# First half products of two dense chunks ahead of their loop, a two-bank integer decode, and later loads from a third buffer

## The chip, the cores and the metric

The program runs on one core of one Trainium2 chip. The metric is the device time in microseconds (us) of one execution, the median of the runs shown. A profiled execution gives the trace; its span runs from the first to the last instruction.

## The reference, cut to what matters

Three stages run one after the other: a linear attention with a decay per channel, a dense layer with an ELU, and a mixture of experts that sends each token to one expert.

```python
def _attn_ref(r, k, v, w, u):                 # (4, 8, 768, 48) each, u (8, 48)
    for t in range(S):
        cur = np.einsum('bhd,bhe->bhde', u[None] * kt, vt)
        y[:, :, t] = np.einsum('bhd,bhde->bhe', rt, state + cur)
        state = wt[:, :, :, None] * state + np.einsum('bhd,bhe->bhde', kt, vt)

def _moe_ref(x, w_in, w_out):                 # x (3072, 384), w_in (384, 2048), w_out (2048, 384)
    h = x @ w_in
    g = np.where(h > 0.0, h, alpha * (np.exp(np.minimum(h, 0.0)) - 1.0))
    return (g @ w_out).astype(np.float32)

def _moe2_ref(x, modality_id, w_gate, modality_bias, w1, w2):
    logits = x @ w_gate + modality_bias[modality_id]
    e_idx = np.argmax(logits, axis=1)
    ...
    for e in range(E):                        # 8 experts, 384 -> 1024 -> 384
        h = np.maximum(x[mask] @ w1[e], 0.0)
        out[mask] = gate_w[mask, None] * (h @ w2[e])
```

`w_in` and `w_out` come in as 64-bit floats and are turned into 32-bit ones on the chip.

## The kernel before, in words

The 3072 tokens are 24 tiles of 128 tokens: tile `i` holds chunk `c` of batch `b`, with `i = 4c + b`. Two tiles make one of 12 groups of 256 tokens.

**Attention** has four steps for each tile. `A1` turns the decays (buffer `lw`) into running products `RK` (a scan on VectorE, L358, then a reciprocal on ScalarE and VectorE, L361 to L364, that works in a PSUM bank). `A2` scales r and k by them (GpSimd, L409). `A3` multiplies them against each other (TensorE, L449) and masks the result (VectorE, L458). `A4` multiplies that with v (L492), adds up `y` (VectorE, L509), splits it into a high and a low half-precision part `x` (ScalarE L516, GpSimd L518) and transposes `x` into `xT` (L385 on TensorE and L386 on ScalarE for tiles 0 to 3, a DMA transpose on SyncE's queue for the others). `upd` keeps the state (L528). From tile 8 on, token rows of r and k (buffer `ld`) take the place of a TensorE product.

**The dense layer** goes through a group's 256 tokens in 8 chunks of 256 hidden columns. `ffn_in(g, u_)` makes 18 products of 256 columns each (L546) into one bank `psf`: two halves `z_` of 128 hidden columns, three parts of the 384 input channels, three products for the high and low parts. ScalarE and VectorE then make the ELU (L553, L554, L555) and ScalarE and GpSimd the two half-precision parts in `ring` (L557, L344). Two units later `ffn_out` multiplies them with `wo` (12 products of 384 columns, L570) into two of the three `pso` banks.

**The weights of the dense layer** come as 16 pieces: 8 of `w_in` and 8 of `w_out`, in the order of `SEQ`: in 0, in 1, in 2, out 0, in 3, out 1, and so on. `prep_` decodes one piece of 768 columns from 64 to 32 bits in six VectorE operations of 384 columns, by way of the bank `pso2` (L292, L293, L294, twice), and ScalarE and GpSimd then scale it and split it (L306, L309, L310). Only group 0 waits for this; the later groups find the weights in place.

**PSUM** has eight banks: two with the tag `f`, three with `a`, and the three `pso`. What `ffn_out` leaves free of a `pso` bank (`SC`) holds small data, such as `Z128`, the decay at the end of a tile (L372, read in L367).

**Order.** The Python code lays the attention steps and the dense units out in one list by the numbers `LEAD`, `LAGS` and `U_`, and a scheduler with a cost model then sets the order on each engine when the kernel is built. At run time each engine takes its instructions strictly in that order. SyncE issues the loads and the DMA transposes from one queue, in order.

Buffers: `psum(tag)` gives the next bank of a tag, `b2`, `p2`, `lw_` and the like are pools with a fixed number of buffers, and a pool that is closed hands its memory to the next one. The pool `LD[0]` is opened after unit 10 in the memory of the decode buffers.

## Time and profile before

| what | before |
|---|---|
| median of 3 runs | 743.87 us (741.7 to 748.42) |
| the profiled execution | 743.09 us |
| its span | 741.3 us |
| granted TensorE clock over the span | 0.993 |
| busy: TensorE, VectorE, ScalarE, GpSimd | 703.3, 506.0, 492.1, 408.3 us |

The profiled execution lasted 743.09 us, of which the span is 741.3 us and 1.79 us lie around it. TensorE is busy for 95% of the span, the others for 55 to 68%. A busy TensorE is not one at its peak, so the waits of TensorE and the spacing of its products tell more than the share.

### The profile page before, as it was taken

Reading aid. Unit: us, or ns where it says so; the run is one execution under the profiler, and the core shown is the slowest. Engines: PE = TensorE matmul, PEld = TensorE weight load, DVE = VectorE, ACT = ScalarE, POOL = GpSimd, SP = SyncE. Lnnn points to the kernel's source line nnn. Section 1 sums busy time; section 2 is a strip of 40 time slices with the busy share of each in tenths; the row PEclk is TensorE's granted clock in tenths of the full one; section 3 lists DMA queues with packets and bytes.
Section 4 is the critical chain, followed back from the end, with each engine's and each line's share of the span. In section 5 each row is a group of like instructions: output and inputs, shape, how many; then the busy total and the mean of one; then the engine's idle time right before and its main releaser. Section 6 shows DMA issues by size and latency. Waiting matters only on the chain.

```text
span 741.3 us, 17669 instructions
## 1 busy us (share of the span) xinstructions
PE 703.3 (95%) x6769; PEld 534.1 (72%) x6769; DVE 506.0 (68%) x1073; ACT 492.1 (66%) x959; POOL 408.3 (55%) x414
## 2 busy tenths in 40 slices
PE   4889999999999999999999999998997999999984
PEld 4767777777777777777777777776775777777763
DVE  5999974575756675657556645776794897667751
ACT  3578875677666677766666755476754887667752
POOL 5878898878677778778767650021053243321221
PEclk9999999999999999999999999999999999999998
DMA  9865442463324442354231201189449999989820
GB/s 301 260 232 188 129 129 66 124 145 86 100 68 105 125 100 69 93 112 98 78 80 56 33 13 34 54 286 275 144 164 284 341 370 330 249 244 272 267 77 13
DMA packets 89059, 114.77 MB, mean 155 GB/s; under 512 B 60709, under 2 KB 67018, under 8 KB 88964
## 3 DMA queue, kind: packets, MB, share of 16 engines
q1 hardware_dynamic: 84512, 102.75, 49.0%
q0 software_dynamic: 3456, 10.24, 4.6%
q8 instruction: 57, 0.93, 0.5%
q10 hardware_dynamic: 996, 0.53, 0.3%
q14 instruction: 38, 0.31, 0.2%
HBM read 90.29 MB, written 9.84 MB: 135 GB/s over the span
## 4 chain that ended last, share of the span: by engine, by line
PE 41%; DMA 18%; issue 13%; DVE 12%; POOL 9%; ACT 7%; POOLq 0%; DVEq 0%; SPq 0%; ACTq 0%
PE psf L546 13%; PE pso L570 13%; DMA out_dram<-ob,idxb 7%; DMA SG<-in_w_dram 4%; PE pso L907 4%; PE psf L887 3%; POOL ring L344 2%; DMA ld<-in_rk_dram 2%; DVE W L877 2%; DVE sti L294 1%; DVE RK L358 1%; PE psa L452 1%; POOL lk L409 1%; DVE pso L292 1%; DVE pso L293 1%
## 5 line engine op out<-in xcount | busy, mean ns | idle before, releaser
L546 PE MATMUL psf<-xT,wi 128*128 128x256 f16 x1728 | 209.3, 274 | 4.0 <-DVE e L555 1.9
L570 PE MATMUL pso<-wo,ring 128*128 128x384 f16 x1152 | 210.2, 326 | 2.0 <-ACT wo L309 0.7
L546 PEld LDWEIGHTS <-wi 128*128 128x128 f16 x1728 | 165.4, 98 | 31.1 <-issue 3.4
L570 PEld LDWEIGHTS <-ring 128*128 128x128 f16 x1152 | 109.8, 98 | 64.6 <-POOL ring L344 1.8
L344 POOL TENSOR_TENSOR ring<-e,ring 128x512 f16<-128x512 f32 x80 | 92.8, 1162 | 52.3 <-ACT ring L557 50.8
L555 DVE SCALAR_TENSOR_TENSOR e<-e,psf 128x512 f32<-128x512 f32 x96 | 65.7, 684 | 76.8 <-ACT e L554 70.9
L907 PE MATMUL pso<-W,gg 128*128 128x384 f16 x624 | 111.7, 326 | 2.5 <-DVE gg L344 1.4
L887 PEld LDWEIGHTS <-W 128*128 128x128 f16 x1008 | 93.6, 99 | 23.1 <-issue 3.8
L557 ACT ACTIVATE ring<-e 128x512 f16<-128x512 f32 x96 | 60.1, 626 | 48.2 <-DVE e L555 48.0
L907 PEld LDWEIGHTS <-gg 128*128 128x128 f16 x624 | 60.3, 98 | 37.1 <-DVE gg L344 2.1
L918 POOL DMA_INDIRECT out_dram<-ob,idxb x20 | 26.0, 1301 | 91.4 <-DVE ob L917 42.6
L553 ACT ACTIVATE e<-psf 128x512 f32<-128x512 f32 x96 | 56.6, 590 | 27.2 <-PE psf L546 23.1
L554 ACT ACTIVATE e<-e,nel 128x512 f32<-128x512 f32 x96 | 69.1, 720 | 2.3
L877 DVE SCALAR_TENSOR_TENSOR W<-SG,W 128x768 f16<-128x768 f32 x56 | 52.8, 956 | 19.2 <-ACT W L875 19.1
L887 PE MATMUL psf<-XM,W 128*128 128x256 f16 (+1 forms) x540 | 62.3, 266 | 1.4 <-ACT mt L893 1.3
L877 DVE SCALAR_TENSOR_TENSOR W<-wi,W 128x768 f16<-128x768 f32 x56 | 52.3, 954 | 13.1 <-ACT W L875 11.9
L875 ACT ACTIVATE W<-SG 128x768 f16<-128x768 f32 x56 | 45.8, 838 | 20.5 <-DMA SG<-in_w_dram 18.9
L344 DVE TENSOR_TENSOR gg<-mt,gg 128x256 f16<-128x256 f32 (+1 forms) x112 | 43.1, 402 | 21.8 <-ACT gg L894 21.0
L875 ACT ACTIVATE W<-wi 128x768 f16<-128x768 f32 x56 | 45.4, 838 | 13.4 <-DMA wi<-in_w_dram 9.9
L893 ACT ACTIVATE mt<-psf 128x256 f32<-128x256 f32 (+1 forms) x84 | 29.4, 360 | 23.7 <-PE psf L887 18.0
L894 ACT ACTIVATE gg<-mt 128x256 f16<-128x256 f32 (+1 forms) x112 | 42.2, 400 | 1.5
L358 DVE TENSOR_TENSOR_SCAN RK<-lw,bnd 112x520 f32<-112x520 f32 x24 | 36.4, 1517 | 7.9 <-ACT lw L357 4.5
(268 smaller groups left out, 1131.9 us busy)
## 6 DMA issues: line engine op xcount, KB each, us to landing
SG<-in_w_dram SPq DMA_DIRECT2D x28, 768.0 KB, 6.7
wi<-in_w_dram SPq DMA_DIRECT2D x28, 768.0 KB, 6.2
stg<-in_w_in_dram SPq DMA_DIRECT2D x8, 768.0 KB, 4.7
stg<-in_w_out_dram SPq DMA_DIRECT2D x8, 768.0 KB, 4.5
ld<-in_rk_dram SPq DMA_DIRECT2D x16, 384.0 KB, 3.2
lw<-in_w_dram SPq DMA_DIRECT2D x24, 227.5 KB, 3.0
lr<-in_r_dram SPq DMA_DIRECT2D x24, 224.0 KB, 2.9
lk<-in_k_dram SPq DMA_DIRECT2D x24, 224.0 KB, 3.0
```

Of the source, the lines that this page charges most:

```text
L344: (nc.gpsimd if pool else nc.vector).tensor_tensor(lo, f, hi, op=ALU.subtract)
L358: nc.vector.tensor_tensor_scan(flat(PR), lw, bnd, 0.0, op0=ALU.mult, op1=ALU.add)
L546: mm = nc.tensor.matmul(ph[:, 256 * z_:256 * z_ + 256], lhsT=wi[:, u_, a, kk, 128 * z_:128 * z_ + 128], rhs=xg[:, b_ * KD + kk, :], start= ...
L553: nc.scalar.activation(e, ph, AF.Exp, scale=_pow2(-PH))
L554: nc.scalar.activation(e, e, AF.Identity, scale=_pow2(PH), bias=nel)
L555: LASTV[0] = nc.vector.scalar_tensor_tensor(e, e, 0.0, ph, op0=ALU.min, op1=ALU.max).ins
L557: LASTA[0] = nc.scalar.activation(hl[:, 0], e, AF.Copy).ins
L570: nc.tensor.matmul(po_[g][i][:, 0:DM], lhsT=hl[:, a, z_, 128 * i:128 * i + 128], rhs=wo[:, u_, b_, z_, :], start=(u_ + z_ + n == 0), stop= ...
L875: nc.scalar.activation(o_[:, 0], i_, AF.Copy, scale=_pow2(sc))
L877: LCV[0] = nc.vector.scalar_tensor_tensor(o_[:, 1], i_, _pow2(sc), o_[:, 0], op0=ALU.mult, op1=ALU.subtract).ins
L887: nc.tensor.matmul(ph[:, 0:n_], lhsT=w_[:, a, kk, 128 * m:128 * m + 128], rhs=xm[:, b_ * KD + kk, 0:n_], start=(n == 0), stop=(n == 3 * KD ...
L907: MK[0] = nc.tensor.matmul(po[:, 0:DM], lhsT=h2[:, a, m, 128 * t:128 * t + 128], rhs=w_[:, b_, m, :], start=(m == 0 and a + b_ == 0), stop ...
```

## The change

Three parts, and what they need:

1. `ffn_half` makes the products of the first 128 tokens of group 0 (tile 0) for dense chunks 0 and 1 ahead of the loop, 18 products of 128 columns each. `ffn_in(0, 0)` and `ffn_in(0, 1)` then make the 18 products for the other 128 tokens into the same bank. Both `f` banks are taken from the first half product on; so `A1` and `A2` of tile 2 and the transposes of tile 1 go to `a` banks.
2. The first six pieces of the weights (`NW2`) are decoded in three VectorE operations of 768 columns over two banks (`psw`). After unit 2 these two banks become `pso1` and `pso2`, and the other ten pieces are decoded as before. `Z128` moves from the free part of `pso1` to that of `pso0`, and `rk` in `route_b` makes room for it.
3. `ld` gets three buffers in place of two, and the decay loads `lw` that are issued once `LD[0]` is open come from three buffers there in place of two of `lw_`.

```diff
+NW2 = 6
...
-    OB = [ps.tile([128, 512], F32, tag=f"o{q}", name=f"pso{q}", bufs=1) for q in range(3)]
-    SC = [t[:, DM:512] for t in OB]
+    OB = [ps.tile([128, 512], F32, tag="o0", name="pso0", bufs=1)]
+    SC = [OB[0][:, DM:512]]
+    pe_ = ctx.enter_context(ExitStack())
+    PW = [pe_.enter_context(tc.tile_pool(name="pw", bufs=1, space=PSUM)).tile([128, 2, 512], F32, name="psw")]
+
+    def open_banks():
+        pe_.close()
+        PW[0] = None
+        pq_ = ctx.enter_context(tc.tile_pool(name="po", bufs=1, space=PSUM))
+        for q in range(1, 3):
+            OB.append(pq_.tile([128, 512], F32, name=f"pso{q}"))
+            SC.append(OB[q][:, DM:512])
...
-    Z128 = SC[1][0:PT, 0:B * QH].rearrange("p (b s) -> p b s", b=B)
+    Z128 = SC[0][0:PT, 64:64 + B * QH].rearrange("p (b s) -> p b s", b=B)
...
-            for o in (0, 384):
-                pt = psum(PDT[0]).bitcast(I32)[:, 0:384]
-                h_, l_ = hi[:, o:o + 384], lo[:, o:o + 384]
+            for o, m_ in ((0, 768),) if PW[0] is not None else ((0, 384), (384, 384)):
+                if PW[0] is not None:
+                    pt = PW[0][:, :, 0:384].bitcast(I32)
+                else:
+                    pt = psum(PDT[0]).bitcast(I32)[:, 0:384].unsqueeze(1)
+                h_, l_, t_ = (x_[:, o:o + m_].rearrange("p (a x) -> p a x", x=384) for x_ in (hi, lo, t))
...
-                t = LD[0].tile([128, 2, DM], F32, tag="ld", name="ld")
+                t = LD[0].tile([128, 2, DM], F32, tag="ld", name="ld", bufs=3)
...
-                t = lw_.tile([PT, 2, QH, HW], F32, tag="lw", name="lw")
+                t = (lw_ if LD[0] is None else LD[0]).tile([PT, 2, QH, HW], F32, tag="lw", name="lw", bufs=2 if LD[0] is None else 3)
...
-        y0 = psum("f" if i < EAR else "a")[0:PT].rearrange("p (r t) -> p r t", t=HF)
+        y0 = psum("f" if i < 2 else "a")[0:PT].rearrange("p (r t) -> p r t", t=HF)
...
-            pk = psum("f" if i < EAR else "a")
+            pk = psum("f" if i < 2 else "a")
...
-        transp(xg[:, :, col:col + 128], x.rearrange("p a c -> p (a c)"), i < NPX)
+        transp(xg[:, :, col:col + 128], x.rearrange("p a c -> p (a c)"), i < NPX, "a" if i == 1 else "f")
...
-    def ffn_in(g, u_):
-        ph = psum("f")
-        xg = xT[g]
-        mm = None
+    HALF = {}
+
+    def ffn_h(ph, g, u_, t0, t1):
         for z_ in range(2):
             n = 0
             for kk in range(KD):
                 for a, b_ in LOHI:
                     mm = nc.tensor.matmul(
-                        ph[:, 256 * z_:256 * z_ + 256], lhsT=wi[:, u_, a, kk, 128 * z_:128 * z_ + 128],
-                        rhs=xg[:, b_ * KD + kk, :], start=(n == 0), stop=(n == 3 * KD - 1),
+                        ph[:, 256 * z_ + t0:256 * z_ + t1], lhsT=wi[:, u_, a, kk, 128 * z_:128 * z_ + 128],
+                        rhs=xT[g][:, b_ * KD + kk, t0:t1], start=(n == 0), stop=(n == 3 * KD - 1),
                     )
                     n += 1
+        return mm
+
+    def ffn_half(u_):
+        HALF[u_] = psum("f")
+        ffn_h(HALF[u_], 0, u_, 0, 128)
+
+    def ffn_in(g, u_):
+        if g == 0 and u_ in HALF:
+            ph = HALF.pop(u_)
+            mm = ffn_h(ph, g, u_, 128, 256)
+        else:
+            ph = psum("f")
+            mm = ffn_h(ph, g, u_, 0, 256)
...
-        rk = scr_(64, nt * E).rearrange("p (t e) -> p t e", e=E)
+        rk = scr_(32, nt * E).rearrange("p (t e) -> p t e", e=E)
...
+    for u_ in range(2):
+        ffn_half(u_)
     mp = mb = None
...
+        if n == LAG:
+            pre(SEQ[NW2 - 1])
+            open_banks()
         if n >= LAG:
```

The scheduler moves instructions on every engine. Three places are shown; a line number of after is 11 to 26 higher than that of the same statement before.

**VectorE at pieces in 2, out 0 and in 3**, where the decode meets tile 1's `y` and the reciprocal of tiles 2 and 3. `stg` is a piece as it came, `sti` the decoded piece, `pso2` and `psw` the banks of the decode, `RK1` the products of the odd tiles. Before:

```order
L458 SCALAR_TENSOR_TENSOR ohp_75<-psa_269,cs_66 128x512
L292 TENSOR_SCALAR pso2_69<-stg_442 128x384
L293 SCALAR_TENSOR_TENSOR pso2_69<-stg_442,pso2_69 128x384
L294 SCALAR_TENSOR_TENSOR sti_444<-stg_442,pso2_69 128x384
L292 TENSOR_SCALAR pso2_69<-stg_442 128x384
L363 SCALAR_TENSOR_TENSOR RK1_104<-RK1_104,psa_468 112x8x64
L293 SCALAR_TENSOR_TENSOR pso2_69<-stg_442,pso2_69 128x384
L364 SCALAR_TENSOR_TENSOR RK1_104<-RK1_104,psa_468 112x8x64
L294 SCALAR_TENSOR_TENSOR sti_444<-stg_442,pso2_69 128x384
L509 SCALAR_TENSOR_TENSOR y_291<-psa_282,dv_280 128x384
```

After:

```order
L472 SCALAR_TENSOR_TENSOR ohp_77<-psa_268,cs_66 128x512
L307 SCALAR_TENSOR_TENSOR psw_71<-stg_471,psw_71 128x2x384
L308 SCALAR_TENSOR_TENSOR sti_473<-stg_471,psw_71 128x768
L306 TENSOR_SCALAR psw_71<-stg_480 128x2x384
L523 SCALAR_TENSOR_TENSOR y_290<-psa_281,dv_279 128x384
L307 SCALAR_TENSOR_TENSOR psw_71<-stg_480,psw_71 128x2x384
L308 SCALAR_TENSOR_TENSOR sti_482<-stg_480,psw_71 128x768
```

Three wide operations stand where six narrow ones stood, and tile 1's `y` (L509, L523 after) no longer has the pair L363, L364 ahead of it.

**TensorE from tile 1's product with v (`ohp` as its operand) to the first dense products.** Rows of `x` are tile 0's transposes, rows of `ohp` under L385 and L399 tile 1's, and `wi` the weights of a dense chunk. Before:

```order
L492 MATMUL psa<-lv,ohp 128x48 x4
L385 LDWEIGHTS x
L385 MATMUL psf<-id_83,x 128x128
...
L385 LDWEIGHTS ohp
L385 MATMUL psf<-id_83,ohp 128x128
...
L546 LDWEIGHTS wi
L546 MATMUL psf<-xT,wi 128x256
...
L449 MATMUL psa<-gg 128x128 x6
```

After:

```order
L506 MATMUL psa<-lv,ohp 128x48 x8
L399 LDWEIGHTS x
L399 MATMUL psf<-id_85,x 128x128
...
L559 LDWEIGHTS wi
L559 MATMUL psf<-xT,wi 128x128
...
L399 LDWEIGHTS ohp
L399 MATMUL psa<-id_85,ohp 128x128
L542 MATMUL psa<-lv,gg 64x48
```

Of the 36 half products, 22 now stand between tile 0's and tile 1's transposes, the other 14 behind tile 1's transposes; then come the 36 products for tile 1.

**SyncE's queue where `LD[0]` opens.** `X` under the transposes is the dense layer's output of group 0. Before:

```order
L340 DMA lv<-in_v_dram 128x384
L340 DMA lw<-in_w_dram 112x520
L380 DMA_TRANSPOSE xT<-x 128x6x128
L340 DMA lw<-in_w_dram 112x520
L331 DMA ld<-in_rk_dram 128x768 x2
L340 DMA lw<-in_w_dram 112x520
L380 DMA_TRANSPOSE xT<-X_107 128x6x128 x2
```

After:

```order
L354 DMA lv<-in_v_dram 128x384
L394 DMA_TRANSPOSE xT<-x 128x6x128
L354 DMA lw<-in_w_dram 112x520 x2
L345 DMA ld<-in_rk_dram 128x768
L354 DMA lw<-in_w_dram 112x520
L345 DMA ld<-in_rk_dram 128x768 x2
L354 DMA lw<-in_w_dram 112x520 x2
L394 DMA_TRANSPOSE xT<-X_109 128x6x128 x2
```

Five decay loads and three row loads stand ahead of the transposes of `X`, where three and two stood; the load for tile 7, which was issued long before, is now among them.

## Rows read from the trace of the kernel before

**Rows 1.** The page: busy time by engine, and TensorE's busy tenths in 40 slices.

```profile
PE 703.3 (95%) x6769; PEld 534.1 (72%) x6769; DVE 506.0 (68%) x1073; ACT 492.1 (66%) x959; POOL 408.3 (55%) x414
...
PE   4889999999999999999999999998997999999984
```

**Rows 2.** TensorE's waits, 0 to 110 us: total us, times, longest us.

```profile
PE psf L385 <- ACT ohp L516: 2.5, 1, 2.5
PE psf L546 <- DVE RK L364: 1.2, 1, 1.2
...
PE psf L546 <- ACT xT L386: 0.9, 1, 0.9
PE pso L570 <- ACT wo L309: 0.7, 1, 0.7
```

**Rows 3.** TensorE's waits, 110 to 490 us, the whole answer.

```profile
PE pso L570 <- POOL ring L344: 0.2, 1, 0.2
```

**Rows 4.** The timeline of TensorE, 0 to 60 us: start us, duration us.

```profile
33.14 0.52 PE L385 MATMUL psf<-id,x 128*128 128x128 f16 x3
36.12 0.50 PE L385 MATMUL psf<-id,ohp 128*128 128x128 f16 x3 [2.46 <-ACT ohp L516]
37.11 0.50 PE L385 MATMUL psf<-id,ohp 128*128 128x128 f16 x3 [0.49 <-POOL ohp L518]
38.51 3.73 PE L546 MATMUL psf<-xT,wi 128*128 128x256 f16 x18 [0.90 <-ACT xT L386]
43.44 2.14 PE L546 MATMUL psf<-xT,wi 128*128 128x256 f16 x18 [1.19 <-DVE RK L364]
```

**Rows 5.** VectorE's groups by line, 11 to 43 us: busy us, mean ns.

```profile
L293 DVE SCALAR_TENSOR_TENSOR pso<-stg,pso 128x384 int32<-128x384 int32 x12 | 6.7, 559 | 0.3
...
L294 DVE SCALAR_TENSOR_TENSOR sti<-stg,pso 128x384 int32<-128x384 int32 x12 | 6.6, 547 | 0.5
...
L458 DVE SCALAR_TENSOR_TENSOR Ab<-psa,cs 128x512 f32<-128x512 f32 x2 | 1.4, 688 | 1.5 <-PE psa L449 1.5
```

**Rows 6.** The page: the costliest groups, a VectorE operation of 768 columns.

```profile
L877 DVE SCALAR_TENSOR_TENSOR W<-SG,W 128x768 f16<-128x768 f32 x56 | 52.8, 956 | 19.2 <-ACT W L875 19.1
```

**Rows 7.** The timeline of VectorE, 36 to 44.5 us.

```profile
37.53 0.56 DVE L293 SCALAR_TENSOR_TENSOR pso<-stg,pso 128x384 int32<-128x384 int32 x1
38.13 0.55 DVE L294 SCALAR_TENSOR_TENSOR sti<-stg,pso 128x384 int32<-128x384 int32 x1
...
41.16 0.56 DVE L293 SCALAR_TENSOR_TENSOR pso<-stg,pso 128x384 int32<-128x384 int32 x1
41.64 0.68 DVE L363 SCALAR_TENSOR_TENSOR RK<-RK,psf 112x512 f32<-112x512 f32 x1
...
42.70 0.68 DVE L364 SCALAR_TENSOR_TENSOR RK<-RK,psf 112x512 f32<-112x512 f32 x1
```

**Rows 8.** The timeline of TensorE, 60 to 110 us.

```profile
65.28 0.34 PE L385 MATMUL psf<-id,x 128*128 128x128 f16 x3
65.46 1.15 PE L546 MATMUL psf<-xT,wi 128*128 128x256 f16 x9
...
75.87 0.48 PE L570 MATMUL pso<-wo,ring 128*128 128x384 f16 x2 [0.66 <-ACT wo L309]
...
85.18 2.14 PE L546 MATMUL psf<-xT,wi 128*128 128x256 f16 x18
```

**Rows 9.** The timeline of GpSimd, 60 to 125 us: the last piece of `wi`.

```profile
81.14 1.66 POOL L310 TENSOR_TENSOR wi<-sti,wi 128x768 f16<-128x768 f32 x1 [1.60 <-ACT wi L309]
```

**Rows 10.** The timeline of ScalarE at two places, 29 to 60 and 85 to 112 us.

```profile
39.53 0.58 ACT L361 ACTIVATE psf<-RK 112x512 f32<-112x512 f32 x1
...
98.44 0.40 ACT L357 ACTIVATE lw<-lw 112x104 f32<-112x104 f32 x1 [0.37 <-DMA lw<-in_w_dram]
```

**Rows 11.** The page: the decay loads, KB each, us from issue to landing.

```profile
lw<-in_w_dram SPq DMA_DIRECT2D x24, 227.5 KB, 3.0
```

**Rows 12.** Windows: us, busy of PE, PEld, DVE, ACT, POOL, PEclk, DMA, GB/s.

```profile
33.00:46.00 13.00, 7.83 (x49) 5.36 (x49) 12.48 (x23) 9.38 (x14) 8.76 (x9) 1.00 0.69 231
```

More of the change, by code (lines that the diff above doesn't have):

```diff
@@ L294, in prep_ @@
                 LASTD[0] = nc.vector.scalar_tensor_tensor(
-                    t[:, o:o + 384], l_, 29, pt, op0=ALU.logical_shift_right, op1=ALU.bitwise_or
+                    t_, l_, 29, pt, op0=ALU.logical_shift_right, op1=ALU.bitwise_or
                 ).ins
```

## The prediction

> **What bounds the kernel now.** I read the page first: TensorE is busy for 95% of the span, and of its 40 slices only the first three, two behind the middle and the last two stand below 9 [rows 1]. So a gain must come from a place where TensorE stands still or runs slowly, and the waits of TensorE name those places. From 110 to 490 us it waits 0.2 us in all [rows 3]: there the time is TensorE's own work. In the first 110 us it waits 2.5 us for tile 1's high part of `x`, 0.9 us for tile 1's `xT`, 1.2 us for an `f` bank that the reciprocal of a later tile holds (released by L364), and 0.7 us for a decoded piece of `wo` [rows 2]. The timeline shows them: three transposes of tile 0 end at 33.66 us (33.14 + 0.52), tile 1's two sets run at 36.12 and 37.11, and the first dense chunk starts at 38.51 [rows 4]. Between 33.66 and 38.51 TensorE does 1.00 us of work and is idle for 2.46 + 0.49 + 0.90 = 3.85 us. The first chunk then takes 3.73 us for 18 products, the second, 1.19 us of waiting later, 2.14 us for the same 18, and ends at 45.58 [rows 4]. The granted-clock column reads 1.00 from 33 to 46 us [rows 12], but 3.73 / 18 = 0.207 us for 256 columns fits the 1.2 GHz level and 0.119 the 2.4 GHz one; before the rise the engine had done short fp32 products, nine transposes and 3.85 us of nothing.
>
> VectorE is the second limit of this stage: from 33 to 46 us it is busy for 12.48 of 13.00 us [rows 12], mostly with the decode. From 11 to 43 us, in which the first six pieces are decoded, its 36 narrow operations take about 20 us, 6.7 for L293, 6.6 for L294, and L292 is like L293 [rows 5]. And the decode is close to TensorE to the end of group 0: TensorE waits 0.66 us for a piece of `wo` at 75.87 [rows 8], and the last piece of `wi` is ready at 82.80 (81.14 + 1.66) [rows 9] for the chunk that starts at 85.18 [rows 8], 2.4 us ahead. So TensorE can only run ahead in this stage if the decode does too.
>
> **The wide decode.** It takes out 36 operations of 384 columns and puts in 18 of 768. A narrow one takes 0.555 us (mean of 0.559 and 0.547), one of 512 columns from PSUM 0.688 [rows 5], so 128 columns more cost 0.13 and 384 more 0.38: 0.94 us by this line, and 0.956 us by an operation of 768 columns elsewhere [rows 6]. I take 0.95. A pair of narrow ones in a row costs 2 x 0.60 us from start to start (37.53 to 38.13) [rows 7], a wide one 0.95 + 0.04 = 0.99, so 0.21 us is saved; 18 pairs make 3.8 us. Where an unrelated operation stands between, the narrow one costs only 0.48 (41.16 to 41.64) [rows 7], a pair 0.96, a wide one no less than 0.88, and 0.08 is saved: 18 x 0.08 = 1.4 us is the low end. No row has an operation over two banks; should each pay another fixed part, narrow's 0.555 less three times 0.13, 0.16 us, the saving is gone (0 to 1 us), which is the low bound. Most narrow ones stand in a row, as in the order shown, so I take 3.2 us by which the decode is earlier from piece 6 on. The ten other pieces keep their six operations and shift as they are.
>
> **The half products.** The order puts 22 of the 36 between tile 0's and tile 1's transposes. At the low rate a half product takes 0.207 / 2 = 0.104 us, 36 of them 3.73 us: they fit the idle 3.85 us nearly exactly. The work they do would else stand behind tile 1. What is left at 38.5 us is 36 half products in place of two full chunks and the bank wait between them: 3.73 us at the low rate, an end at 42.24 in place of 45.58, **3.3 us earlier**. At the high rate it is 2.14 us, an end at 40.65, 4.9 us earlier. I take the low rate, since the trace shows it up to the middle of the first chunk and the rise may come no sooner. Tile 1's own chain has room both ways. By the order its `y` stands behind 13 wide operations (13 x 0.99 = 12.9 us) in place of 24 narrow ones (24 x 0.60 = 14.4 at most) and no longer behind L363 and L364 (0.68 each [rows 7]): up to 2.9 us earlier on VectorE. But its transposes stand behind 22 half products, 2.3 us at the low rate, so on TensorE it gains little: 0 to 1.1 us, and I take 0.
>
> Splitting costs something by itself. At the high rate 18 products take 2.14 and 9 take 1.15 [rows 8], so one is 0.110 us and the tail 0.16; three 128-column transposes take 0.34 [rows 8], which leaves 0.06 for each, against 0.055 for half a product. 72 halves in place of 36 products cost 72 x 0.005 = 0.4 us, half of it in the idle time: 0.2 us, inside the rounding. The Trainium skill, "TensorE: Matmul & The Clock Gate", section "Back-to-back issue gap", speaks against the split: it gives about 81 ns for each 128-column product in a stream where every product has its own weight load. By the Trainium skill's figure an estimate for the 36 second halves is 2.9 us in place of 2.14 at the high rate, and nothing changes at the low one, where 0.104 is longer anyway; the transposes here, each with its own weight load, are on the side of 0.06.
>
> **The two together.** Earlier products without earlier weights would meet the waits on `wo` and `wi` at 70 to 100 us, earlier weights without earlier products would leave TensorE where it is. The halves give 3.3 us, the decode 3.2 with a reserve of 2.4 at the last `wi`: so 3.3 us reach the stretch behind 110 us, where nothing waits, and shift the rest as a whole.
>
> **Bank tags and `Z128`: nothing.** That both `f` banks are held from the first half on is covered by moving tile 2's reciprocal to an `a` bank, and if that cover fails the price is the slower rival's below. `psw` must be given up before the first `ffn_out` writes `pso1`; the sixth piece was decoded by 42.8 us before, beside L364 at 42.70 [rows 7], and by the order the first L570 comes after both chunks and other work, so over 3 us of cover remain. `Z128` and `rk` move from one shared bank to another of the same use.
>
> **Third buffers: nothing.** TensorE has no wait from 110 to 490 us that they could remove [rows 3]. The load for tile 7 is issued later than before, which is the second rival.
>
> **Rivals.** *More (chance 0.17).* The 22 halves in one run raise the rate sooner, the second halves go at the high rate, and tile 1 is 1.1 us earlier: 4.9 + 1.1 = 6.0 us, which the decode just allows (3.8 + 2.4). That is 743.87 - 6.0 = 737.9. For it: the rise came during the first run of dense products; against it: the run is cut by tile 1's transposes. The Trainium skill, "TensorE: Matmul & The Clock Gate", section "What's actually happening", has the slow level as the default that activity ends; by that rule the earlier work in the idle time favours this rival, and the trace agrees so far as the rise came in the first long run.
>
> *Given back (0.18).* Where `LD[0]` opens, SyncE now issues five decay loads and three row loads ahead of the transposes of `X`, and ScalarE, which is in order, stops at L357 until a load lands, 3.0 us after its issue [rows 11]; before it stopped for 0.37 us there [rows 10]. One full landing in which no ELU is made and both `f` banks stay full takes 3.0 of the 3.3 us: 743.6. For it: tile 7's load was long in place before. Against it: of the waits of TensorE in [rows 2] none lies behind 76 us, although ScalarE stood still there too.
>
> *Slower (0.07).* `A1` holds its PSUM bank from 39.53 [rows 10] to 43.38 (42.70 + 0.68) [rows 7], 3.85 us. With both `f` banks taken, tiles 2 and 3 each hold one of three `a` banks while L449 needs two and `A4` one or more. If TensorE waits such a hold out for both tiles, 7.7 us are lost and 3.3 won: 743.87 + 4.4 = 748.3. It decides from 3.3 us of waits on `psa` between 35 and 60 us. Against it: tile 3 used an `a` bank before, and the rows show no such wait.
>
> *No effect (0.06).* The wide operations save nothing (a fixed part for each bank), and the halves then meet the decode, so that only the wait of 0.66 us and the like goes: 743.2.
>
> **How the numbers follow.** The sum against the profiled execution is 743.09 - 3.3 = 739.8 us (span 738.0). That execution lies 0.8 us under the median of 743.87, so the forecast on the median's scale is 740.6 us, chance 0.52. The range goes from 737.0, which takes in most of the first rival and the high end of the decode, to 745.5, which takes in the second and the fourth with the spread of the runs shown (741.7 to 748.42); the third and the far half of the first are left out. One per cent, 7.4 us, is about what a measurement of this kernel can tell from no change. Under 736.4 lies only a part of the first rival, 0.09; above 751.3 a worse form of the third or a loss in a stretch whose order changed unseen, 0.07; the rest, 0.84, is within 1%.
>
> **What would show it.** Right: operations of 768 columns at 0.95 us, and the sixth piece decoded by about 39.5 us; half products in the gap before tile 1's transposes; chunk 1 complete at about 42 us; TensorE's waits in the first 110 us shorter by about 3 us; every landmark behind 110 us earlier by 3 us. Wrong: wide operations over 1.1 us, waits on `psa` before 60 us, waits for the ELU between 90 and 115 us, or a gain before 50 us that is no longer there at 110 us.

## The result and the profile after

The changed kernel takes 752.47 us (median of 8 runs, 750.23 to 755.44), the kernel before, run beside it, 746.62 us (8 runs, 741.7 to 748.84). The ratio is **1.0077, 95% interval 1.0047 to 1.0106**: 0.8% slower, where 0.4% faster was forecast. The ratios here and below are not quotients of the medians: they leave out two slower executions each of e5, e9 and e13 (experiments, below), which the medians include. The profiled execution of the changed kernel lasted 751.55 us, its span 749.7. That is 8.4 us more than the span of the trace before; the medians are 5.9 us apart, because the profiled execution of before was one of its faster ones.

The profile's line numbers have moved (each experiment has its own; e7 those of before): the decode's L292 to L294 are now L306 to L308, its L309 and L310 are L323 and L324, the scale and scan L357 and L358 are L371 and L372, the reciprocal's L363 and L364 are L377 and L378, `Z128`'s L372 is L386, the dense products L546 and L570 are L559 and L596, the transposes and their copies L385 and L386 are L399 and L400, GpSimd's part of `ring` L344 is L358, the ELU's last step on VectorE L555 is L581, and the evacuation of the output products (copying them out of their bank), L578 on ScalarE and L579 on VectorE, is L604 and L605.

The page of the changed kernel: busy time, TensorE's tenths and the granted clock.

```profile
PE 707.1 (94%) x6805; PEld 538.0 (72%) x6805; DVE 506.0 (67%) x1055; ACT 493.0 (66%) x959; POOL 411.7 (55%) x414
...
PE   4999999999999999999999999999998999999984
...
PEclk9999998999999999999999999999999999999998
```

Beside [rows 1] the second and third slices went from 8 to 9: TensorE is better used at the front. But the span has grown, so the time was lost behind it.

**The front does what it was meant to.** VectorE's groups by line in the changed kernel, shapes kept apart, 11 to 43 us (busy us, mean ns):

```profile
L306 DVE TENSOR_SCALAR psw<-stg 128x768 int32<-128x768 int32 x6 | 5.7, 956 | 0.5 <-DMA stg<-in_w_in_dram 0.4
L307 DVE SCALAR_TENSOR_TENSOR psw<-stg,psw 128x768 int32<-128x768 int32 x6 | 5.7, 953 | 0.1
L308 DVE SCALAR_TENSOR_TENSOR sti<-stg,psw 128x768 int32<-128x768 int32 x6 | 5.7, 943 | 0.3 <-POOL wi L324 0.2
```

An operation over two banks takes 0.943 to 0.956 us, as one of 768 columns did elsewhere [rows 6]. The timeline of VectorE has the end of the sixth piece:

```profile
36.30 0.95 DVE L308 SCALAR_TENSOR_TENSOR sti<-stg,psw 128x768 int32<-128x768 int32 x1
```

The sixth piece is decoded at 37.25 us (36.30 + 0.95); before it was 42.8. The timeline of GpSimd has the last piece of `wi`:

```profile
77.30 1.65 POOL L324 TENSOR_TENSOR wi<-sti,wi 128x768 f16<-128x768 f32 x1 [1.81 <-DVE RK L378]
```

It is ready at 78.95 us, before at 82.80 [rows 9]. The timeline of TensorE, 28 to 52 us:

```profile
31.00 0.52 PE L399 MATMUL psf<-id,x 128*128 128x128 f16 x3
32.68 2.51 PE L559 MATMUL psf<-xT,wi 128*128 128x128 f16 x22 [1.16 <-ACT xT L400]
34.98 0.53 PE L399 MATMUL psa<-id,ohp 128*128 128x128 f16 x3
...
36.70 0.96 PE L559 MATMUL psf<-xT,wi 128*128 128x128 f16 x14
37.90 1.05 PE L434 MATMUL psa<-u,rkp 112*128 112x2 f32 x8 [0.24 <-DVE RK L378]
38.81 2.17 PE L559 MATMUL psf<-xT,wi 128*128 128x128 f16 x36
```

The 22 first halves fill the idle time ahead of tile 1's transposes, at 2.51 / 22 = 0.114 us each; the next 14 take 0.069 and the last 36, in a run of their own, 0.060 us each (all with the tail of their run). Two chunks are complete at 40.98 us (38.81 + 2.17), before at 45.58 [rows 4]: 4.6 us earlier. TensorE's waits to 110 us, behind one of 9.7 us at the start that stood in before too; of those of [rows 2] only the one on `xT` is left (1.2 us, before 0.9); the other two below are new:

```profile
PE psf L559 <- ACT xT L400: 1.2, 1, 1.2
PE psa L463 <- DVE RK L378: 1.0, 1, 1.0
PE pso L596 <- ACT pso L261: 0.5, 1, 0.5
```

**Behind 100 us it is lost, and more.** The ELU's last step on VectorE (L555, after L581) runs once for each of the 96 chunks; its start is a milestone. From the traces, us:

| start of | before | after | e1 | e7 | e14 | e12 | e8 |
|---|---|---|---|---|---|---|---|
| ELU 9 | 98.0 | 93.7 | 96.2 | 99.2 | 100.5 | 98.7 | 97.7 |
| ELU 17 | 143.3 | 142.8 | 140.6 | 144.2 | 147.6 | 143.9 | 140.9 |
| ELU 25 | 178.7 | 185.4 | 182.7 | 187.1 | 184.5 | 181.8 | 179.5 |
| ELU 49 | 294.9 | 304.8 | 300.6 | 307.6 | 306.1 | 297.4 | 294.8 |
| ELU 85 | 462.9 | 470.9 | 467.0 | 474.9 | 474.0 | 464.7 | 460.4 |
| first expert product | 510.8 | 518.4 | 515.6 | 524.7 | 524.2 | 513.3 | 508.1 |

(e1, e7, e8, e12 and e14 are experiments, below.) The changed kernel is 4.3 us ahead at ELU 9, 0.5 ahead at ELU 17, 6.7 behind at ELU 25 and 9.9 behind at ELU 49. TensorE's waits from 110 to 490 us, where before had 0.2 us [rows 3]:

```profile
PE pso L596 <- DVE X L605: 3.0, 3, 1.3
PE pso L596 <- POOL ring L358: 2.5, 2, 1.7
PE psa L440 <- ACT dg L436: 1.2, 1, 1.2
PE psa L522 <- ACT kf L442: 0.8, 2, 0.6
PE pso L596 <- DVE ohp L701: 0.5, 1, 0.5
```

There are two stretches of loss. The first is 97 to 124 us. In the timeline of ScalarE:

```profile
101.73 0.39 ACT L371 ACTIVATE lw<-lw 112x104 f32<-112x104 f32 x1 [4.72 <-DMA lw<-in_w_dram]
```

and in the windows of TensorE (us, PE busy, granted clock, DMA share, GB/s):

```profile
100.00:112.00 12.00, 10.49 (x79) 1.00 0.98 238
112.00:116.00 4.00, 3.81 (x25) 0.79 0.20 57
116.00:120.00 4.00, 4.00 (x41) 0.50 0.03 5
120.00:124.00 4.00, 4.00 (x27) 0.85 0.75 97
```

ScalarE waits for a decay load, TensorE is idle for 1.5 us of 12, and then its clock falls to half; before it was granted 1.00 throughout. By these rows the lower clock alone is worth about 3.4 us of full-clock time, an estimate: (0.21 + 0.50 + 0.15) x 4. The second stretch is the larger one. The windows from 140 to 300 us, of before with all engines (busy PE, PEld, DVE, ACT, POOL, then clock, DMA share, GB/s), then of after with TensorE alone:

```profile
140.00:300.00 160.00, 159.70 (x1812) 119.77 (x1812) 103.52 (x216) 109.69 (x209) 124.56 (x136) 1.00 0.40 102
```

```profile
140.00:300.00 160.00, 153.57 (x1748) 1.00 0.36 95
```

TensorE's idle time went from 0.3 to 6.4 of 160 us, at the full clock.

### The profile page after: what moved, and what is told of

Read it like the earlier page. It is cut to its first block, busy times and chain, and to the rows that moved or that the text cites. A ratio compares the mean times of both kernels' runs of the same rounds, so it can differ in the third digit from the quotient of the medians.

```text
span 749.7 us, 17710 instructions
## 1 busy us (share of the span) xinstructions
PE 707.1 (94%) x6805; PEld 538.0 (72%) x6805; DVE 506.0 (67%) x1055; ACT 493.0 (66%) x959; POOL 411.7 (55%) x414
## 4 chain that ended last, share of the span: by engine, by line
PE 51%; DMA 17%; DVE 13%; ACT 7%; issue 6%; POOL 5%; SPq 0%; DVEq 0%; ACTq 0%; POOLq 0%
PE psf L559 15%; PE pso L596 14%; PE pso L933 6%; DMA out_dram<-ob,idxb 6%; PE psf L913 6%; DMA lw<-in_w_dram 3%; DMA wi<-in_w_dram 3%; DMA ld<-in_rk_dram 3%; DVE RK L372 2%; DVE W L903 2%; DMA SG<-in_w_dram 2%; PE psa L913 1%; PE psa L463 1%; DVE e L581 1%; ACT e L580 1%
## 5 line engine op out<-in xcount | busy, mean ns | idle before, releaser
L596 PE MATMUL pso<-wo,ring 128*128 128x384 f16 x1152 | 212.7, 327 | 6.9 <-DVE X L605 3.0
L559 PE MATMUL psf<-xT,wi 128*128 128x256 f16 (+1 forms) x1764 | 211.9, 274 | 2.8 <-DVE e L581 1.6
L559 PEld LDWEIGHTS <-wi 128*128 128x128 f16 x1764 | 167.8, 99 | 29.5 <-issue 3.2
L596 PEld LDWEIGHTS <-ring 128*128 128x128 f16 x1152 | 109.9, 98 | 69.6 <-issue 6.1
L358 POOL TENSOR_TENSOR ring<-e,ring 128x512 f16<-128x512 f32 x80 | 95.2, 1191 | 59.9 <-ACT ring L583 58.7
L581 DVE SCALAR_TENSOR_TENSOR e<-e,psf 128x512 f32<-128x512 f32 x96 | 65.5, 683 | 88.4 <-ACT e L580 80.6
L579 ACT ACTIVATE e<-psf 128x512 f32<-128x512 f32 x96 | 56.4, 589 | 25.5 <-PE psf L559 23.5
L903 DVE SCALAR_TENSOR_TENSOR W<-SG,W 128x768 f16<-128x768 f32 x56 | 52.8, 954 | 16.3 <-ACT W L901 16.2
L358 DVE TENSOR_TENSOR gg<-mt,gg 128x256 f16<-128x256 f32 (+1 forms) x112 | 42.9, 401 | 28.2 <-ACT gg L920 27.2
L903 DVE SCALAR_TENSOR_TENSOR W<-wi,W 128x768 f16<-128x768 f32 x56 | 52.1, 952 | 12.3 <-ACT W L901 11.1
L372 DVE TENSOR_TENSOR_SCAN RK<-lw,bnd 112x520 f32<-112x520 f32 x24 | 37.7, 1572 | 12.3 <-ACT lw L371 8.7
```

What stands on the lines that cost most here:

```text
L358: (nc.gpsimd if pool else nc.vector).tensor_tensor(lo, f, hi, op=ALU.subtract)
L372: nc.vector.tensor_tensor_scan(flat(PR), lw, bnd, 0.0, op0=ALU.mult, op1=ALU.add)
L559: mm = nc.tensor.matmul(ph[:, 256 * z_ + t0:256 * z_ + t1], lhsT=wi[:, u_, a, kk, 128 * z_:128 * z_ + 128], rhs=xT[g][:, b_ * KD + kk, t0: ...
L579: nc.scalar.activation(e, ph, AF.Exp, scale=_pow2(-PH))
L581: LASTV[0] = nc.vector.scalar_tensor_tensor(e, e, 0.0, ph, op0=ALU.min, op1=ALU.max).ins
L596: nc.tensor.matmul(po_[g][i][:, 0:DM], lhsT=hl[:, a, z_, 128 * i:128 * i + 128], rhs=wo[:, u_, b_, z_, :], start=(u_ + z_ + n == 0), stop= ...
```

## The experiments

All ratios are to the kernel before, run beside each kernel on the same chip; in brackets the 95% interval. "Idle" is TensorE's idle time between 140 and 300 us of the profiled execution, 160 less its busy time.

**First suspicion: the third buffers.** The wait of 4.7 us on a decay load was the rival "given back". Four runs take the third part apart.

e1, the change without part 3:

```diff
-                t = LD[0].tile([128, 2, DM], F32, tag="ld", name="ld", bufs=3)
+                t = LD[0].tile([128, 2, DM], F32, tag="ld", name="ld")
...
-                t = (lw_ if LD[0] is None else LD[0]).tile([PT, 2, QH, HW], F32, tag="lw", name="lw", bufs=2 if LD[0] is None else 3)
+                t = lw_.tile([PT, 2, QH, HW], F32, tag="lw", name="lw")
```

> The changed kernel without its third part: ld and lw are back at two buffers each, lw in its old pool. Theory (late decay loads): in the changed kernel the decay loads from tile 7 on wait until the decode's memory is free at 97.0 us, ScalarE stands still for 4.72 us behind the first of them, and everything lost behind 94 us comes from that. Then this kernel keeps the 4.4 us that the changed one was ahead at the ninth ELU: ratio to before 0.992 to 0.996, no ScalarE wait on a decay load over 1 us, TensorE's waits from 100 to 200 us under 1 us. Rival (the new order as such): the halves and the wide decode put attention work ahead of dense work, and the waits behind 110 us come from that; then the ratio stays at 1.003 to 1.009 and TensorE still waits 4 to 5 us from 100 to 200 us.

Measured: 752.22 us, 1.0060 [1.0026, 1.0095], idle 5.1.

e2, the kernel before with these two lines of part 3 alone:

> The kernel before with the third part alone: decay loads issued once the pool is open come from three buffers there, token rows from three. Theory (late decay loads): the loads wait for the decode's memory, which comes free at about 101 us here, ScalarE stands still 3 to 5 us, and the loss of the changed kernel behind 94 us is there without its gain: ratio 1.010 to 1.018. Rival (the new order as such): no loss from these loads, ratio 0.998 to 1.003.

Measured: 747.74 us, 1.0000 [0.9968, 1.0031], idle 2.1.

e3, the change with the decay rows back in their old pool (the second of the two lines undone):

> The changed kernel with the decay loads back in their old pool of two buffers, the token rows at three. Theory (late decay loads): as without the whole third part, ratio 0.992 to 0.997. Second theory (the rows): three token-row loads in the same rush share the DMA engines and cause the late landing; then this kernel keeps part of the loss, ratio 0.999 to 1.004. Rival (the new order as such): 1.003 to 1.009.

Measured: 755.11 us, 1.0105 [1.0038, 1.0172], idle 6.5.

e4, the change with two buffers for the token rows (the first of the two lines undone):

> The changed kernel with the token rows back at two buffers, the decay loads from three in the late pool. Theory (late decay loads): no better than the changed kernel, ratio 1.004 to 1.010, and ScalarE still waits 3 us or more for the first late decay load. Second theory (the rows): with one row load less in the rush the wait falls below 2 us, ratio 0.995 to 1.000.

Measured: 756.78 us, 1.0103 [1.0037, 1.0168], idle 5.8.

The suspicion falls: the third buffers alone cost nothing, and without them parts 1 and 2 lose 0.6%.

**Second: which of parts 1 and 2, and is it the move of `Z128`?** New waits of TensorE named the first shared bank's scratch (`pso L596 <- ACT pso L386`, 0.3 us in e1, is the write of `Z128`). So `Z128` and `rk` were treated as a fourth part.

e5, before with the 128-token products and their bank tags alone (`ffn_h`, `ffn_half`, the two calls, `i < 2` for `i < EAR`):

> The kernel before with only the 128-token products of the first two dense chunks (and the bank tags that make room for them); decoding in pairs of 384 columns, the scratch places and the pools as before. Theory of the shared bank (the loss of parts 1 and 2 comes from the Z128 scratch and the ranks, which the change puts into the bank that holds the logits and takes the output products of every third tile): this run has none of that, so it keeps the front gain; 0.2 to 0.5% faster than before, about 743.5 to 745 beside 746.6, and its E operations of ELU #16 to #48 stay ahead of those of before. Rival, the new order as such (dense products started earlier push the attention chain and the products wait for their tokens later): 0.3 to 0.7% slower, already between ELU #16 and #24.

Measured: 755.49 us, 1.0087 [1.0047, 1.0127], idle 1.7.

e6, before with the wide decode alone, which brings the move of `Z128` and `rk`:

> The kernel before with only the wide decode of the first six chunks, which needs two free banks and so moves Z128 and the ranks into the bank of the logits; no 128-token products, pools as before. Theory of the shared bank: carries the whole loss of parts 1 and 2, 0.5 to 0.9% slower, with waits of the output products on that bank's scratch between 100 and 490 us. Rival, the new order as such: near no change, within 0.3%, since the first products of the dense part start when they did before and the decode merely ends sooner.

Measured: 755.72 us, 1.0103 [1.0052, 1.0153], idle 7.7.

e7, before with that move and nothing else:

```diff
-    Z128 = SC[1][0:PT, 0:B * QH].rearrange("p (b s) -> p b s", b=B)
+    Z128 = SC[0][0:PT, 64:64 + B * QH].rearrange("p (b s) -> p b s", b=B)
...
-        rk = scr_(64, nt * E).rearrange("p (t e) -> p t e", e=E)
+        rk = scr_(32, nt * E).rearrange("p (t e) -> p t e", e=E)
```

> The kernel before with two places changed and nothing else: Z128 moves from the second shared bank into the first one, at the columns that the change gives it, and the ranks move inside it to make room. Same operations, same number of instructions. Theory of the shared bank: 0.4 to 0.9% slower, most of the loss without any of the gain, and the output products wait for the write of Z128 or for the routing scratch after 100 us. Rival, the new order as such: within 0.3% of before.

Measured: 756.75 us, 1.0101 [1.0054, 1.0148], idle 7.4.

e8, e1 with `Z128` in SBUF:

```diff
-    Z128 = SC[0][0:PT, 64:64 + B * QH].rearrange("p (b s) -> p b s", b=B)
+    Z128 = p1.tile([PT, B * QH], F32, name="Z128").rearrange("p (b s) -> p b s", b=B)
```

> The changed kernel without its third buffers (1.006 of before in its run), and with Z128 in a small SBUF tile of its own in place of the first shared bank. Theory of the shared bank: the products of the first shared bank no longer wait for attention scratch, so the front gain is kept, 0.3 to 0.6% faster than before (742 to 744.5 beside 746.6). Rival, the new order as such: 0.4 to 0.8% slower than before, as the kernel without the third buffers was.

Measured: 745.39 us, **0.9967 [0.9936, 0.9999]**, idle 1.6.

Three of the four answers are the shared bank's: two lines that move 16 columns of scratch into that bank, and the ranks within it, cost 1.0%, and taking `Z128` out of the bank turns 1.0060 into 0.9967. The stops are even the same. TensorE's timeline in the changed kernel, and then in e7, which has none of its halves or wide operations:

```profile
174.72 1.80 PE L596 MATMUL pso<-wo,ring 128*128 128x384 f16 x10 [1.67 <-POOL ring L358]
...
190.93 1.78 PE L596 MATMUL pso<-wo,ring 128*128 128x384 f16 x10 [1.32 <-DVE X L605]
...
232.88 1.14 PE L596 MATMUL pso<-wo,ring 128*128 128x384 f16 x6 [1.27 <-DVE X L605]
```

```profile
175.40 1.80 PE L570 MATMUL pso<-wo,ring 128*128 128x384 f16 x10 [1.49 <-POOL ring L344]
...
193.62 3.36 PE L570 MATMUL pso<-wo,ring 128*128 128x384 f16 x10 [2.30 <-DVE X L579]
...
236.00 1.14 PE L570 MATMUL pso<-wo,ring 128*128 128x384 f16 x6 [0.94 <-DVE X L579]
```

Three stops for the same two reasons, each 0.7 to 3.1 us later in e7. The fourth answer, e5, is not the bank's: it loses 0.9% without the move. Its waits, 40 to 140 us (L582 is the output product):

```profile
PE pso L582 <- ACT wo L309: 2.3, 1, 2.3
PE pso L582 <- POOL wo L310: 1.8, 2, 0.9
```

and its windows:

```profile
60.00:72.00 12.00, 10.21 (x66) 0.72 0.63 200
...
120.00:132.00 12.00, 12.00 (x78) 0.57 0.23 60
```

Dense products that start earlier, with a decode that doesn't, stop for pieces of `wo`, 4.1 us where before stopped for 0.7 [rows 2], and the clock is low in both windows.

**Third: is the own tile good by itself, or only against the bank?** An edit can also change the order that the scheduler finds elsewhere, so `Z128` was given its own tile (the diff of e8) in four more kernels.

e9, before with the own tile:

> The kernel before, with Z128 in a small SBUF tile of its own in place of the second shared bank; nothing else changed. Theory of the coupling (attention scratch that shares a bank with the output products makes the products, their evacuation and the attention steps wait for one another; parts 1 and 2 lose by it, and it is worst in the bank of the logits): the kernel before has little of it (0.2 us of waits of TensorE between 110 and 490 us), so within 0.3% of before. Rival, the lucky order (each edit re-deals the whole order of instructions, and the kernel before is a good draw): anything from -0.3 to +1%, most likely 0.5% slower, as three of the draws so far.

Measured: 751.41 us, 1.0053 [1.0014, 1.0091], idle 1.1.

e10, e5 with the own tile:

> The 128-token products alone (1.0087 of before with Z128 in the second shared bank), with Z128 in an SBUF tile of its own. Theory of the coupling: the loss goes, 0 to 0.4% faster than before (745 to 748 beside 748), TensorE's waits between 100 and 490 us under 2 us. Rival, the lucky order: 0.5 to 1% slower as without the own tile, or anywhere between.

Measured: 753.70 us, 1.0107 [1.0076, 1.0137], idle 2.8. It still stops 3.1 us for pieces of `wo` between 40 and 140 us, and the window of 60 to 72 us is granted 0.57:

```profile
60.00:72.00 12.00, 9.95 (x49) 0.57 0.50 168
```

e11, e6 with the own tile:

> The wide decode of six chunks alone (1.0103 of before with Z128 in the bank of the logits), with Z128 in an SBUF tile of its own; the ranks stay where the change puts them. Theory of the coupling: the loss goes, 0 to 0.4% faster than before. Rival, the lucky order: 0.5 to 1% slower, or anywhere between.

Measured: 747.89 us, 1.0015 [0.9989, 1.0042], idle 1.1.

e12, the whole change with the own tile:

> The whole change, third buffers too (1.0077 of before), with Z128 in an SBUF tile of its own. Theory of the coupling: 0.2 to 0.6% faster than before, like the same without the third buffers (0.9967). Rival, the late decay loads that come with the third buffers (a 4.7 us wait of ScalarE at 101.7 us and a fall of TensorE's clock behind it in the changed kernel): 0.3 to 0.6% slower than before. Rival, the lucky order: anywhere from -0.3 to +1%.

Measured: 747.00 us, 1.0007 [0.9983, 1.0031], idle 2.6.

From the first shared bank to the own tile three kernels gain: e6 to e11 by 0.9%, the change to e12 by 0.7%, e1 to e8 by 0.9%. From the second shared bank to the own tile two don't: before to e9 loses 0.5%, e5 to e10 shows no change (their intervals overlap). So it isn't PSUM as such. e11 and e12 come out level with before and not faster, as the theory had it, and e10 slower, for its own reason. e9 also misses what the theory expected of it, and sets a bound: an edit with next to no work in it can move this kernel by half a per cent (e9 counts five runs).

**Fourth: what of that bank?** The first shared bank differs from the second in holding the logits and the routing's scratch. e13 and e15 leave `Z128` there and move the routing out; e14 brings both together in the other bank, in the kernel before.

e13, the whole change, and e15, e1, both with:

```diff
-        lgt[t0 // RT_] = SC[0][:, 0:RT_ * E].rearrange("p (t e) -> p t e", e=E)
+        lgt[t0 // RT_] = SC[1][:, 0:RT_ * E].rearrange("p (t e) -> p t e", e=E)
...
-        t = SC[0][:, o:o + n]
+        t = SC[1][:, o:o + n]
```

> The whole change (1.0077 of before) with Z128 left in the first shared bank, and the logits and the routing's scratch moved out of it into the second one. Theory of the two scratches (attention's Z128 and the routing's logits, counts and ranks in one bank order the two against each other, and with the products of that bank; it costs whichever bank it is): as with Z128 in a tile of its own, 0.998 to 1.004 of before, and TensorE idle between 140 and 300 us falls from 6.4 to under 3 us. Rival, the products' bank (Z128 beside the output products is the cost, the routing has no part): stays at 1.005 to 1.010 with over 5 us idle there.

Measured: 752.20 us, 1.0035 [1.0000, 1.0069], idle 2.4.

> The changed kernel without its third buffers (1.006 of before), Z128 left in the first shared bank, the logits and the routing's scratch moved into the second one. Theory of the two scratches: as with Z128 in a tile of its own (0.9967), 0.994 to 1.000 of before. Rival, the products' bank: stays at 1.004 to 1.008.

Measured: 749.72 us, 1.0040 [1.0006, 1.0073], idle 0.2.

e14, before with the same two lines, `Z128` at `SC[1][0:PT, 64:...]`, `rk` at `scr_(32, ...)`, and the gate's `m1` and `m0` in `SC[0]`:

> The kernel before with the logits and the routing's scratch moved into the second shared bank, beside Z128, which stays there (at the columns 64 and up), and the two short-lived vectors of the gate's preparation moved the other way. Theory of the two scratches: 0.5 to 1% slower, as when Z128 went to the routing's bank (1.0101), with 5 us or more of TensorE idle between 140 and 300 us. Rival, the products' bank: within 0.3% of before.

Measured: 755.56 us, 1.0095 [1.0063, 1.0127], idle 6.8.

e14 is the clearest: in the other bank, without a move of `Z128` out of it, the company of the routing's scratch costs 0.95%. In e13 and e15 the idle time goes as expected, but e15 missed its range and stands at the lower edge of its rival's, and e13 reaches only the upper part of its own. Their times alone don't tell: the intervals overlap with those of e1 and of the change.

**Fifth: through which wait?** In the changed kernel ScalarE waits six times for a load of decay rows between 140 and 300 us:

```profile
ACT lw L371 <- DMA lw<-in_w_dram: 11.2, 6, 4.0
```

and the chain at 228 to 233 us reads like the cause. The timelines of VectorE, then SyncE's queue, then ScalarE of the changed kernel:

```profile
226.69 1.60 DVE L372 TENSOR_TENSOR_SCAN RK<-lw,bnd 112x520 f32<-112x520 f32 x1 [0.69 <-ACT pso L386]
...
232.27 0.56 DVE L605 SCALAR_TENSOR_TENSOR X<-pso,X 128x384 f16<-128x384 f32 x1 [2.12 <-ACT X L604]
```

```profile
228.32 0.33 SPq L354 DMA_DIRECT2D lw<-in_w_dram  x1
```

```profile
231.47 0.40 ACT L371 ACTIVATE lw<-lw 112x104 f32<-112x104 f32 x1 [2.12 <-DMA lw<-in_w_dram]
231.76 0.48 ACT L604 ACTIVATE X<-pso 128x384 f16<-128x384 f32 x1
```

The scan waits for the write of `Z128` (L386), the next decay load is issued when the scan ends (226.69 + 1.60 = 228.29), ScalarE waits for it, the evacuation L604 stands behind that on ScalarE, L605 behind L604, and TensorE's stop at 232.88 ends with L605. The programs with both scratches in one bank (after, e1, e3, e4, e6, e7, e14) have six such waits each, 7.4 to 13.6 us together; the others up to here have one to three, 0.4 to 6.3 us. Three runs took the wait off ScalarE:

```diff
-        nc.scalar.activation(lw[:, DB0::DBL], lw[:, DB0::DBL], AF.Copy, scale=2.0)
+        if LD[0] is None:
+            nc.scalar.activation(lw[:, DB0::DBL], lw[:, DB0::DBL], AF.Copy, scale=2.0)
+        else:
+            nc.vector.tensor_scalar(lw[:, DB0::DBL], lw[:, DB0::DBL], 2.0, None, op0=ALU.mult)
```

e16, in the whole change:

> The whole change (1.0077 of before), with the doubling of the decay rows moved from ScalarE to VectorE, right ahead of the scan that reads them, for the steps behind the ELU part's eighth product (from about 100 us on); the earlier steps as they were. Z128 stays beside the routing's scratch. Theory of the chain (the two scratches in one bank let the scan, and so the load that reuses its buffer, come late; ScalarE stands 11.2 us in six waits for that load between 140 and 300 us, the evacuations behind it on ScalarE come late, and TensorE waits for them): ScalarE no longer waits there, TensorE idle in 140 to 300 us falls from 6.4 to under 4 us, 1.000 to 1.004 of before. Rival, ScalarE's waits are a by-product: 1.006 to 1.010, idle over 5 us.

Measured: 759.17 us, 1.0188 [1.0157, 1.0219], idle 6.7.

e17, in the kernel before:

> The kernel before with the doubling of the decay rows moved from ScalarE to VectorE in the same way; control for the run on the changed kernel. Theory of the chain: before has two such waits, 3.9 us together, and TensorE idle 0.3 us of 160, so nothing is to be won: within 0.4% of before. Rival, a by-product: the same.

Measured: 750.59 us, 1.0065 [1.0038, 1.0093], idle 3.4.

e18, in e8:

> The changed kernel without its third buffers and with Z128 in a tile of its own (0.9967 of before), with the doubling on VectorE too. Theory of the chain: that kernel has no wait of ScalarE for a decay load between 140 and 300 us, so nothing more is to be won, 0.994 to 1.000 of before. Rival, a by-product: the same; this run is the candidate for a version that beats both.

Measured: 749.01 us, 1.0038 [1.0017, 1.0059], idle 1.5.

All three missed. The wait did not go away, it went to VectorE; the waits of VectorE in e16 and then in e18, 140 to 300 us (L374 is the doubling there):

```profile
DVE lw L374 <- DMA lw<-in_w_dram: 13.0, 7, 2.8
```

```profile
DVE lw L374 <- DMA lw<-in_w_dram: 12.3, 6, 2.8
```

The two wait alike for the load, but TensorE is idle for 6.7 us in e16 and for 1.5 in e18, where `Z128` is alone. So the late decay load is one link at one of the stops, not the cause of the idle time; the chain above shows how one stop came about, no more. (e18's expectation says that e8 has no such wait of ScalarE; its trace has one, of 0.8 us.)

**What the traces show of the order.** The order on VectorE can be read off directly. Its timeline around the 21st ELU step (L555), first of the kernel before, then of e7, which has the same lines and operations (L604 writes the logits, L626 to L647 are the routing's steps, L367 reads `Z128`, L358 is the scan):

```profile
159.26 0.68 DVE L555 SCALAR_TENSOR_TENSOR e<-e,psf 128x512 f32<-128x512 f32 x1
159.86 0.15 DVE L367 SCALAR_TENSOR_TENSOR dmc<-RK,pso 112x4 f32<-112x4 f32 x1
...
160.70 1.24 DVE L358 TENSOR_TENSOR_SCAN RK<-lw,bnd 112x520 f32<-112x520 f32 x1
161.86 0.17 DVE L626 TENSOR_REDUCE mx<-pso 128x4 f32<-128x32 f32 x1
```

```profile
162.51 0.68 DVE L555 SCALAR_TENSOR_TENSOR e<-e,psf 128x512 f32<-128x512 f32 x1
...
163.91 0.19 DVE L626 TENSOR_REDUCE mx<-pso 128x4 f32<-128x32 f32 x1
...
166.28 0.18 DVE L647 TENSOR_TENSOR o<-pso,km 128x32 f16<-128x32 f32 x1
166.38 0.15 DVE L367 SCALAR_TENSOR_TENSOR dmc<-RK,pso 112x4 f32<-112x4 f32 x1
...
169.76 1.95 DVE L358 TENSOR_TENSOR_SCAN RK<-lw,bnd 112x520 f32<-112x520 f32 x1
```

Before, the step that reads `Z128` and the next scan stand ahead of the routing's steps; in e7 they stand behind all of them, and the scan starts 7.25 us after the start of this ELU step in place of 1.44. Scans come late wherever the two scratches share a bank: counted on VectorE, the 12th, 14th, 16th and 20th of the 24 scans stand behind 22 or 23, 30, 38 or 39, and 55 ELU steps in all eight such programs, and behind 21, 29, 37 and 53 in all twelve others. In seven of the eight (not e14, whose stops are spread over later chunks) 2.6 to 4.9 us of TensorE's stops fall between the ELU steps 21 and 27, in the twelve others 0 to 1.3.

## Why the prediction was wrong, point by point

**What bounds the kernel: right.** TensorE's own work is the time behind 110 us, so every stop that appears there is paid in full: of the 8.5 us lost between ELU 17 and ELU 85 (0.5 ahead, then 8.0 behind) 7.0 are additional idle time of TensorE from 140 to 500 us (7.4 us against 0.4 before, by the windows).

**The wide decode: right, undersized.** Operations at 0.95 us, as taken; no further fixed part for the second bank. The sixth piece came 5.5 us earlier (37.25 against 42.8) where 3.2 was forecast, the last `wi` 3.85. The operations themselves give 2.9 of the 5.5 us (3 x 5.7 = 17.1 us, beside some 20 [rows 5]); the rest is other work and idle time that no longer stands ahead of the sixth piece, which the forecast did not count.

**The half products: right, undersized.** 22 of them fill the gap. The end at 40.98 us lies between the forecast's 42.24 and the first rival's 40.65, because the last 36 went at 0.060 us each and not at 0.104: that the rate rises sooner was the first rival's mechanism, and it held. The Trainium skill, "TensorE: Matmul & The Clock Gate", section "Back-to-back issue gap", gives about 81 ns for them; the trace disagrees.

**The two together: right.** Halves without the earlier decode lose 0.9% (e5) and 1.1% (e10), the decode without the halves gives nothing (e11, 1.0015), both together with no other cost give 0.33% (e8, without part 3; 0.01 to 0.64%), 2.5 us of the forecast's 3.3. That this is the lead of the front, carried through, is not shown: in the trace of e8 the lead is 2.4 us at ELU 17 and 2.7 us at the first expert product, but -0.8 and 0.1 us at ELU 25 and 49, and the expert stage behind it takes 4.1 us longer than before's (508.1 to 742.7 us beside 510.8 to 741.3), at a granted clock of 0.98 against 0.99 (490 to 735 us).

**Bank tags and `Z128`: nothing. This is the step that failed.** "`Z128` and `rk` move from one shared bank to another of the same use" counted only the output products as the bank's use. The first bank also holds the logits and the routing's scratch, and scratch of two stages that otherwise have nothing to do with each other in one bank costs this kernel about 1% where it was brought together (e7, e14), and parting it gave 0.7 to 0.9% back where `Z128` got its own tile (e12, e11, e8, each against its own kernel) and 0.2 and 0.4%, within the noise, where the routing moved (e15, e13). With both in one bank, whichever it was, TensorE idled 5.1 to 7.7 us between 140 and 300 us in all eight programs (after, e1, e3, e4, e6, e7, e14, e16); with the two apart, 0.2 to 3.4 us in the twelve others. The step had the move in the text and priced it at zero without asking who else touches the new bank.

What this does to the program can be said in part. The Trainium skill, "PSUM — Partial Sum Buffer", section "PSUM bank collisions raise a hardware error", says that different engines may not touch one bank in the same quarter of the partitions at the same time, at other columns either, and that such accesses have to be kept apart by semaphores. The traces agree that they are: output products into columns 0 to 383 wait for ScalarE's write of `Z128` into the columns behind (0.3 us in e1, 0.4 in e3, 0.5 in e14, 0.6 in e6, 1.5 in e16, none in the twelve programs with the two apart; before 495 us). These direct waits are small. The larger part is the order of the instructions: e7 has the operations of before, every one, and stops where before doesn't, for evacuations and `ring` that come late. The traces show the order that goes with the shared bank in all eight programs and in none of the twelve others: the step that reads `Z128`, and the scan behind it, are set one or two dense chunks late, behind routing steps that they precede elsewhere. That TensorE's stops come of this order is argued from the pairs and from where the stops lie; e16 to e18 were meant to show the link and did not. Whether the tie is one of the bank or of the program's buffer stays open too: in every run both scratches were slices of the same tile (`OB[0]` or `OB[1]`) when they shared a bank. The order is set when the kernel is built, so it could have been read before any run; the prediction looked only at places in the first 100 us or so.

**"Shift the rest as a whole": wrong by the same step.** Order changes behind 110 us were in the forecast only as a remark with a part of 0.07.

**Third buffers: nothing. Right for the measure** (e2, 1.0000; e1 beside the whole change is no different within the intervals). With `Z128` alone e12 is 0.4% slower than e8, but their intervals overlap. The rival "given back" had its mechanism, a decay load that ScalarE waits 4.7 us for, and its signs came up (a lead of 4.3 us at ELU 9, of 0.5 at ELU 17), but it isn't what decides: e1 has no third buffers and about the same loss. In the traces the first stretch of loss is not in e1 (1.8 us ahead at ELU 9, 2.7 at ELU 17), but e12, which has the third buffers, was granted 1.00 from 100 to 140 us as well, where the changed kernel was granted 0.91.

**The other rivals.** "Slower" needed waits on `psa` of over 3.3 us between 35 and 60 us; there were 1.2 (1.0 and 0.2). "No effect" needed wide operations without a saving; they saved. "More" was near on the end of the halves (40.65, measured 40.98), but nothing of that lead was left at ELU 25.

What stays open besides: e9, which should have moved nothing, is 0.5% slower, and e13 and e15, which part the scratches, stop at 1.004 where the own tile reaches 0.997 to 1.001. e17, 0.65% slower, is no case of a new order: instruction by instruction its VectorE has 1072 of before's 1073 in the same order and its ScalarE 941 of the 942 that it keeps, so its loss goes with the moved doubling. e16 is slower than the change by 1.1% with the same idle time; why stays open. Single pairs of half a per cent prove nothing here; the cause named above rests on the pairs that agree (e7, e14, e6 with e11, e1 with e8, the change with e12) and on the order.

## What to carry to other kernels

Ask of each buffer that a change moves who else uses the memory it moves to, bank by bank and not column by column: a few columns of scratch, placed beside the scratch of another stage, cost more here (up to 1.0%) than the wide decode and the half products together brought (0.3%). A tile of its own for such a small, long-lived value gave 0.7 to 0.9% back here where it parted two stages' scratch; in the kernel before, where they were apart already, it cost 0.5%. Where a scheduler sets the order when the kernel is built, compare the whole order before and after, behind the place that was changed too, before forecasting half a per cent.

## What the runs showed of the hardware that was not expected

- A run of 128-column half-precision products, each with its own weight load, took 0.060 us each in the changed kernel (2.17 us for 36, its tail included; by this spacing at the 2.4 GHz level), about half of a 256-column product (2.14 us for 18 [rows 4]): splitting them cost next to nothing.
- VectorE's operations over two PSUM banks cost what operations of the same length cost elsewhere (0.943 to 0.956 against 0.954 us for L903 of the changed kernel).
- One idle stretch can cost twice: in the changed kernel 1.5 us of idle time between 100 and 112 us were followed by granted clocks of 0.79, 0.50 and 0.85 in the next three windows of 4 us, and with the stops of e5 and e10 the window of 60 to 72 us was granted 0.72 and 0.57.
